# Three shift products of a fused long-convolution kernel: sums by accumulating DMA, one more inverse by eight, a borrowed gate buffer

## The chip, the cores and the metric

The program runs on one core of one Trainium2 chip. The metric is the device time of one execution in microseconds; the figure that counts is the median of several executions. Engines are named as the profile names them: PE (matmul), PEld (its weight loads), DVE, ACT, POOL, SP. SP, ACT and POOL also issue the DMAs.

## What is computed

Forward and backward of one block, sequence S = 2048, width D = 1024, hidden width F = 3584, all in bf16:

```python
xn = layernorm(q)
k_shift = sum_t k_pad[:, t:t+S, :] * shift_k[:, 3 - t]      # causal, four taps
kv = k_shift * v
y  = irfft(rfft(kv, 2S) * rfft(ssm_k, 2S))[:S] + kv * ssm_D   # long convolution
s  = xn * y
g  = silu(((xn @ w_gate) * (xn @ w_up)) @ w_down)
out = q + s * g
# outputs: out, and the gradients of q, k, v, shift_k, ssm_k, ssm_D and the three weights
```

The long convolution is done by matmuls with tables of sines and cosines (transforms of 128 points) and butterfly sums on DVE.

## The kernel before, in words

**The first 505 us** hold the part that the change touches. Two streams run interleaved there.

The *gate stream* multiplies xn by the gate and up weights. F is cut into NSL = 14 slabs of 256 columns; a slab is done in four *units* of 512 rows (`gu_unit`, L692; `turned_unit`, L664, for the slabs in `TURNED` = 2 to 6, 12, 13). A unit is four groups of eight 128x512 matmuls. Each group goes to one of two PSUM buffers (`psg`) and is copied by ACT to one half-row of a tile `gut`; after the fourth group ACT stores `gut` to DRAM (`GTd` or `GUd`). The product of the two halves (`multiply`, output `hN`, three buffers) is given to DVE after the first group of the next unit. A `gut` tile is free when its product is done and its store has landed. `gut_tile` (L658) hands them out: pool `fg` has two, and every third unit of slabs below 12 takes half of `U[5]` as a third. The last eight units are slab 12 rows 0 and 512, slab 13 rows 0 and 512, slab 12 rows 1024 and 1536, slab 13 rows 1024 and 1536; they are called units 1 to 8 below. In slabs that are not turned, pairs of `hN` are transposed on PE and copied by ACT to a tile `hT` (one buffer, pool `fg`), which SP stores (`turn_pair`, L730); the call is put off by five groups, so that of slab 11's last pair falls into unit 2.

The *convolution stream* is the generator `conv_forward` (L775). It goes over eight slices `ds` of 128 channels: transforms of the filter and of kv (PE matmuls to `psF`, ACT copies to `SP`, DVE sums `W`, `KX`, `HX`), the spectra's product on DVE, an inverse on DVE, and its last matmuls (`tail`, output `psI`). The inverse is `inv_dft` (L375), or `inv8` (L403) for slices in `INV8` = 4 to 7; `inv8` has more sums on DVE and leaves half as many matmuls to `tail`. For each pair of slices, `shift(dp)` (L793) makes kv: seven products and sums over 128x4096 elements on DVE and an eighth product with v. For dp = 1, 2, 3 it runs in one piece in the odd slice before, between the spectra's product and the inverse, with its inputs k and v loaded by `load_kv` at that slice's start; acc is `U[6]`, prod is `U[7]`, v is `U[4]`.

The order is fixed when the program is built. After each group, `tick` (L1020) advances the generator until the sum of its yielded weights reaches its share of `F_TOTAL`; a group of a turned slab counts `TURNED_TICK` = 0.958. DVE instructions of the convolution stay in program order (`PIN`), and every engine runs its own list in order. What is left of the convolution goes on beside the first matmuls of the next stage (`bm_first`, output `psbm`), up to about 560 us.

**After that** come the down projection, the gates' gradients, and the backward matmuls and convolutions, which the change does not touch. Late in them stands the one accumulating DMA that the kernel has: four times 1 MB from q onto out (L1772), DRAM to DRAM, issued by POOL.

Of the kernel before, what the change touches and what calls it, by code (L numbers as in the profile page):

```python
# [13 lines left out]
BF16 = mybir.dt.bfloat16  # L14
# [5 lines left out]
def build_kernel(  # L20
# [11 lines left out]
    nc = tc.nc  # L32
    P = 128
    _, S, D = A_q.shape
    F = B_w_gate.shape[1]
    assert (S, D, F) == (2048, 1024, 3584) and A_shift_k.shape[1] == 4
    NB = S // P
# [3 lines left out]
    NSL = F // SLW  # L41
# [16 lines left out]
    ADD, SUB, MUL = ALU.add, ALU.subtract, ALU.mult  # L58
# [6 lines left out]
    def st(out, in_):  # L65
        ins = nc.gpsimd.dma_start(out=out, in_=in_)
        if PINQ[0]:
            tc.keep_in_program_order(ins)
        return ins
# [6 lines left out]
    def cld_k(t, c, dp):  # L76

        rows = lambda u, n, a: bass.AP(kin.tensor, kin.offset + (1024 * c + 8 * u - 3 + a) * D + dp * 256,
                                       [[8 * D, n], [D, 11 - a], [1, 256]])
        for u, n, a in ((0, P, 0),) if c else ((16, P - 16, 0), (1, 15, 0), (0, 1, 3)):  # L80
            cld(t[u:u + n, a:], rows(u, n, a))
# [5 lines left out]
    def pool(name, bufs=1, side=None, space=None):  # L87
        kw = dict(name=name, bufs=bufs, reuse_waits="tile")
        if side:
            kw["side"] = side  # L90
        if space is not None:
            kw["space"] = space
        return tc.alloc_tile_pool(**kw)
# [10 lines left out]
    KSHd = dram.tile([4, P, NB, 256], BF16, name="KSHd")  # L104
# [9 lines left out]
    TURNED = (2, 3, 4, 5, 6, 12, 13)  # L114
# [16 lines left out]
    Wbc = const.tile([P, 4, D], BF16, name="Wbc")  # L131
# [77 lines left out]
    def pinned(ins):  # L209
        if PIN[0]:  # L210
            tc.keep_in_program_order(ins)
        newest[0] = ins

    def tt(o, a, b, op):
        pinned(V.tensor_tensor(o, a, b, op))  # L215
# [250 lines left out]
    def rowps(ps):  # L466
        return ps[:].rearrange("p r (c d) -> p r c d", c=2)
# [47 lines left out]
    U = [ua.tile([P, 4096], BF16, name=f"U{i}") for i in range(8)]  # L515
# [6 lines left out]
    fg = pool("fg", 2, side="right")  # L522
# [13 lines left out]
    kst = pool("kst", 1)  # L536
# [116 lines left out]
    turn_of = [0]  # L653
# [3 lines left out]

    def gut_tile(sl):  # L658
        turn_of[0] += 1
        if turn_of[0] % 3 == 0 and sl < NSL - 2:  # L660
            return U[5][:, 2048:4096].rearrange("p (a i f) -> p a i f", a=2, i=4)
        return fg.tile([P, 2, 4, SLW], BF16, name="gut")[:]

    def turned_unit(sl, b0, w, tick):  # L664
# [3 lines left out]
        for j in range(2):  # L668
            for a in range(2):
# [7 lines left out]
                hn[0] = nop  # L677
                tick(TURNED_TICK)
        cols = slice(b0 * P, b0 * P + 512)
# [85 lines left out]
    cv_gone = []  # L765
    ht_st = [None]
    EIGHT = ((0, 0), (0, 1), (6, 0), (7, 0), (7, 1))
    INV8 = (4, 5, 6, 7)
    SHIFT_W = 8 * 2.3

    conv_state = {"forward": True, "filters": True}
# [3 lines left out]
    def conv_forward():  # L775
        S_ = conv_state

        def load_kv(dp, c):
            S_["k", dp] = krow
            if dp > 0 or c == 0:  # L780
                for i in range(2) if dp == 0 else (c,):
                    cld_k(krow[:, i], i, dp)
            if dp > 0 or c == 1:
                for i in range(2) if dp == 0 else (c,):
                    v = U[4][:, 2048 * i:2048 * i + 2048].rearrange("p (a x) -> p a x", a=8)
                    cld_v(v, i, dp * 256, 256)
# [6 lines left out]
        def shift(dp):  # L793
            kv = cx.tile([P, NB, 256], BF16, name="kv")
            S_["kvt", dp] = kv
            k = S_.pop(("k", dp))
            wb = lambda j: Wbc[:, j:j + 1, dp * 256:(dp + 1) * 256].unsqueeze(1).to_broadcast([P, 2, 8, 256])
            room = cx.tile([P, 16, 256], BF16, name="KX")[:].rearrange("p a x -> p (a x)") if dp == 0 else U[7][:]
            acc, prod, v = [t.rearrange("p (c r d) -> p c r d", c=2, r=8) for t in (U[6][:], room, U[4][:])]
            with tc.issue_after(last.ins):  # L800
                tt(acc, k[:, :, 0:8, :], wb(3), MUL)
            yield 2.3
            for j in (2, 1, 0):
                tt(prod, k[:, :, 3 - j:11 - j, :], wb(j), MUL)
                yield 2.3
                tt(acc, acc, prod, ADD)
                yield 2.3
            tt(kv[:].rearrange("p (c r) d -> p c r d", c=2), acc, v, MUL)
            st(KSHd[dp], U[6][:].rearrange("p (b d) -> p b d", b=NB))
            yield 2.3  # L810
# [22 lines left out]
        def tail(ds):  # L833
# [5 lines left out]
            for rq in range(2):  # L839
                ps = (ps_tr if cv_gone else ps_cv).tile([P, 4, 256], F32, name="psI", tag="tr" if cv_gone else "psF")  # L840
                inv_quad(G, ps, rq, ds in INV8)
                pe_us[0] += 0.9 if ds in INV8 else 1.8
                nc.scalar.copy(out=yf.rearrange("p (c r) d -> p r c d", c=2)[:, 4 * rq:4 * rq + 4], in_=rowps(ps))
# [10 lines left out]
        cx = pool("cx", 1)  # L854
        cs = pool("cs", 1)
# [45 lines left out]
        sp = [half(0, S_["hx"], i, Dz[:, 0:P]) for i in range(2)]  # L901
        for ds in range(8):
            yield 0.5
            if ds % 2 == 1 and ds < 7:
                with tc.issue_after(S_["kst"].ins):
                    for c in range(2):
                        load_kv(ds // 2 + 1, c)
            D0 = Dz[:, ds * P:(ds + 1) * P]
            sph = []
            KX = cx.tile([P, 16, 256], BF16, name="KX")  # L910
            HX = cs.tile([P, 16, 256], BF16, name="HX", bufs=2)
            own_room = lambda X: X[:].rearrange("p a x -> p (a x)").bitcast(F32).rearrange("p (a x) -> p a x", a=8)[:, 0:4]
            eight = (ds, 1) in EIGHT
            if ds == 0:
                yield from transform(0, 1, sp, HX, own_room(KX), lambda i: sph.append(half(0, kvs(0), i)), nop)
            else:
                yield from transform(ds, 0, sp, KX, own_room(HX), lambda i: sph.append(half(ds, S_["hx"], i, D0)), nop)
                S_["kst"] = st(KFd[ds], KX[:])
            calls = []

            def behind():
                calls.append(0)
                if len(calls) % 2 == 0:
                    next(tl, None)
            room = cf.tile([P, 4, 256], F32, name="room", tag="hx")[:] if eight else None
            yield from transform(ds, int(ds > 0), sph, HX if ds else KX, room, nop1 if eight else lambda c: h_rows(ds + 1, c),
                                 behind)
            if ds == 0:
                S_["kst"] = st(KFd[0], KX[:])
            if eight:  # L930
                h_rows(ds + 1, 0)
            turned(HX, 1, 0, 1)
            yield 1.3
            if eight:
                h_rows(ds + 1, 1)
            if ds == 7:
                cf.release()
                S_["filters"] = False
            st(HFd[ds], HX[:])
            yield from product(KX, HX, KX, cs, False, 0)  # L940
            if ds % 2 == 1 and ds < 7:
                yield from shift(ds // 2 + 1)
            sp = []

            def ahead():
                if ds < 7:
                    sp.append(half(ds + 1, kvs(ds + 1), len(sp)))
            yield from (inv8 if ds in INV8 else inv_dft)(KX, HX, cs, ahead if ds % 2 == 0 else None, ahead)
            if ds % 2 == 1:
                ahead()  # L950
            S_["G", ds] = HX
            tl = tail(ds)
# [5 lines left out]
        kst.release()  # L958

    F_TOTAL = 4 * SHIFT_W + 3.0 + 8 * (0.5 + FWD4_W + 1.3 + PROD_W + INV_W) + 10.0 - 0.95 * 8 * (4 * 1.75 + 0.95 + 4 * 0.9)  # L960
    F_TOTAL += len(EIGHT) * (FWD8_W - 9.6 + 0.95 * 1.75) - 2.0
    F_TOTAL += len(INV8) * (INV8_W - INV_W + 0.95 * 1.8)
    conv = conv_forward()
# [50 lines left out]
    ps_cv = pool("ps_cv", 2, space=PSUM)  # L1014
    pump, drain, step = make_pump(conv, F_TOTAL)
    cnt = [-5]
    TURNED_TICK = 0.958
    NT = 24 * 8.0 + 33 - 16 * len(TURNED) * (1 - TURNED_TICK)

    def tick(by=1):  # L1020
        cnt[0] += by
        if cnt[0] == -4:
            pump((SHIFT_W + 4.05) / F_TOTAL)
        if cnt[0] >= -2:
            pump((SHIFT_W + (F_TOTAL - SHIFT_W) * (cnt[0] + 6.5) / (NT + 3.5)) / F_TOTAL)

    pump((SHIFT_W + 3.95) / F_TOTAL)
    for i_ in (4, 5):
# [267 lines left out]
    bpump, bdrain, _ = make_pump(conv_backward(), C_TOTAL)  # L1296
# [169 lines left out]
    for bp in range(2, 8):  # L1466
# [6 lines left out]
        with tc.issue_after(row_ld[0].ins):  # L1473
            if bp in (4, 5, 7):
                q = (4, 5, 7).index(bp)
# [206 lines left out]
    kpump, kdrain, _ = make_pump(dk_units(kw_), DK_TOTAL)  # L1682
# [70 lines left out]
    for g in range(1, 4):  # L1753
        for b in (4 * g, 4 * g + 2):
            end = b == NB - 2
            pss = [ps_x.tile([P, D], F32, name="psx") for i in range(2)]
            for n in range(12 if end else 14):
# [11 lines left out]
                elif b == NB - 4 and n in (0, 3, 6, 9):  # L1769
                    rows = slice(512 * (n // 3), 512 * (n // 3) + 512)  # L1770
                    with tc.issue_after(gu_mm[0].ins):
                        tc.keep_in_program_order(nc.gpsimd.dma_start(out=out_0.flatten_outer_dims()[rows, :],  # L1772
                                                                     in_=A_q.flatten_outer_dims()[rows, :], accum_op=ADD,
                                                                     max_dma_last_dim=4096))
# [82 lines left out]
```

## Time and profile before

| what | us |
|---|---|
| median of 3 executions | 1908.94 |
| the 3 executions | 1908.68, 1908.94, 1914.21 |
| the profiled execution, its own time | 1916.02 |
| its span, first to last instruction | 1914.2 |
| PE busy in 60 to 505 us (of 445) | 436.6 |
| DVE busy in 60 to 505 us (of 445) | 435.8 |
| PE busy in 560 to 1914 us (of 1354) | 1342.6 |

A "wait" below is idle time of an engine together with what ended it, as the profile infers it from semaphores. "Landing" is the time from a DMA's issue to its completion. The profiled execution is one execution; times inside it are counted from its first instruction.

### The profile page before, as it was taken

To read this page: it belongs to the slowest core of one execution; us is meant where nothing else is said; L and a number is where in the kernel's file an instruction comes from. 1 tells how busy PE (TensorE), PEld (TensorE's weight loads), DVE (VectorE), ACT (ScalarE), POOL (GpSimd) and SP (SyncE) were. 2 spreads that over 40 slices of the span, in tenths; PEclk is the share of its full clock that TensorE was granted. 3 is DMA by queue.
4 is the path that set the end of the run, shared out by engine and by line. 5 is a ranking of instruction groups with operands and counts; after the bars stand their busy time and mean duration, and the time that the engine had idled before them with its cause. 6 is when DMAs were issued, how large, how long until landed. Compare 5 with 4: busy or idle time off the path is not lost.

```text
span 1914.2 us, 27244 instructions
## 1 busy us (share of the span) xinstructions
PE 1886.6 (99%) x10815; PEld 1009.5 (53%) x10947; DVE 1544.5 (81%) x1701; ACT 611.7 (32%) x899; POOL 334.9 (17%) x465
## 2 busy tenths in 40 slices
PE   8999999999999999999999999999999999999998
PEld 4554555544444466666666656664444444444443
DVE  8999999999977546887999999999995206788843
ACT  5754545555232234332222222222222002011112
POOL 5121212101113210001021221211212101121121
PEclk9999999999999999999999999999999999999999
DMA  8777867759759998778987798685988999998997
GB/s 296 269 256 249 253 211 235 239 195 315 268 198 329 294 307 230 193 205 240 230 269 241 236 274 243 197 287 163 249 221 190 215 203 192 190 185 187 193 214 124
DMA packets 524447, 444.29 MB, mean 232 GB/s; under 512 B 356096, under 2 KB 451996, under 8 KB 512544
## 3 DMA queue, kind: packets, MB, share of 16 engines
q1 hardware_dynamic: 459680, 239.04, 51.0%
q0 software_dynamic: 41152, 174.15, 29.1%
q10 hardware_dynamic: 23488, 29.36, 4.4%
q8 instruction: 85, 1.39, 0.3%
q14 instruction: 42, 0.34, 0.1%
HBM read 171.85 MB, written 189.84 MB: 189 GB/s over the span
## 4 chain that ended last, share of the span: by engine, by line
PE 61%; DVE 11%; issue 9%; DMA 6%; POOL 1%; ACT 1%; SPq 0%; POOLq 0%; DVEq 0%; ACTq 0%
PE psb L1550 20%; PE psb L1533 10%; PE psb L1626 9%; PE psbm L1070 9%; PE psx L1688 7%; PE psg L672 3%; DMA dkT<-DKSHd 2%; DVE dkp L1285 2%; DMA dxna_t<-DXNAd 1%; PE psF L237 1%; DVE W L215 1%; DVE KX L215 1%; DVE dxn L215 1%; DVE HX L215 1%; DVE m L215 1%
## 5 line engine op out<-in xcount | busy, mean ns | idle before, releaser
L1550 PE MATMUL psb<-U,U 128*128 128x512 bf16 x1792 | 397.1, 379 | 0.0
L1688 PE MATMUL psx<-U,dgut 128*128 128x512 bf16 x1505 | 331.0, 379 | 1.6
L1688 PEld LDWEIGHTS <-dgut 128*128 128x128 bf16 x1792 | 175.3, 98 | 211.4
L1550 PEld LDWEIGHTS <-U 128*128 128x128 bf16 x1792 | 175.2, 98 | 198.0
L1533 PE MATMUL psb<-wdt,U 128*128 128x256 bf16 x1792 | 205.6, 273 | 0.0
L706 PE MATMUL psg<-wslab,U 128*128 128x512 bf16 x867 | 198.9, 379 | 5.5 <-DMA wslab<-in_B_w_gate_dram 2.4
L672 PE MATMUL psg<-U,wslab 128*128 128x512 bf16 x869 | 198.1, 381 | 3.7 <-ACT gut L674 2.3
L1533 PEld LDWEIGHTS <-U 128*128 128x128 bf16 x1792 | 175.2, 98 | 29.2
L215 DVE TENSOR_TENSOR W<-W 128x1024 f32<-128x1024 f32 (+1 forms) x183 | 180.3, 1002 | 4.0
L1626 PE MATMUL psb<-U,U 128*128 128x512 bf16 x797 | 176.1, 379 | 0.9
L1285 DVE SCALAR_TENSOR_TENSOR dkp<-dkT,kT 128x1024 bf16<-128x1024 bf16 (+2 forms) x64 | 78.3, 1224 | 115.9 <-DMA dkT<-DKSHd 114.1
L1555 ACT CAST wb<-psb 128x512 bf16<-128x512 f32 x112 | 65.6, 586 | 315.5 <-PE psb L1550 315.5
L1070 PE MATMUL psbm<-U,ht 128*128 128x512 bf16 x658 | 145.0, 379 | 0.7
L1626 PEld LDWEIGHTS <-U 128*128 128x128 bf16 x896 | 87.4, 98 | 104.3
L672 PEld LDWEIGHTS <-wslab 128*128 128x128 bf16 x896 | 87.4, 98 | 101.4 <-issue 3.4
L706 PEld LDWEIGHTS <-U 128*128 128x128 bf16 x896 | 86.1, 98 | 100.6 <-issue 3.0
L1720 ACT ACTIVATE dx_t<-dxn 128x1024 bf16<-128x1024 f32 x15 | 15.9, 1057 | 331.3 <-DVE dxn L215 331.3
L215 DVE TENSOR_TENSOR U<-U,dht 128x2048 bf16<-128x2048 bf16 x56 | 68.3, 1221 | 49.1 <-ACT dht L1535 48.9
L1070 PEld LDWEIGHTS <-ht 128*128 128x128 bf16 x672 | 65.7, 98 | 78.1
L1535 ACT CAST dht<-psb 128x512 bf16<-128x512 f32 x112 | 65.6, 587 | 116.2 <-PE psb L1533 115.9
L674 ACT CAST gut<-psg 128x512 bf16<-128x512 f32 x88 | 51.5, 587 | 87.5 <-PE psg L672 83.0
L1667 ACT CAST wbs<-psb 128x512 bf16<-128x512 f32 x51 | 29.9, 586 | 145.4 <-PE psb L1626 131.4
(268 smaller groups left out, 2456.1 us busy)
## 6 DMA issues: line engine op xcount, KB each, us to landing
DGd<-U SPq DMA_DIRECT2D x28, 1024.0 KB, 5.0
U<-GUd SPq DMA_DIRECT2D x14, 1024.0 KB, 9.7
out_dram<-wb SPq DMA_DIRECT2D x112, 128.0 KB, 3.7
GTd<-gut ACTq DMA_DIRECT2D x22, 512.0 KB, 5.1
ht<-HTd SPq DMA_DIRECT2D x18, 512.0 KB, 7.6
GUd<-gut ACTq DMA_DIRECT2D x17, 512.0 KB, 6.3
KFd<-KX POOLq DMA_DIRECT2D x8, 1024.0 KB, 4.9
HFd<-HX POOLq DMA_DIRECT2D x8, 1024.0 KB, 7.3
```

The costliest lines, as they stand in the source:

```text
L215: pinned(V.tensor_tensor(o, a, b, op))
L672: gu_mm[0] = nc.tensor.matmul(ps[:], w[:, dc, a, j * P:(j + 1) * P], XNT[b0 // 4][:, dc, :], start=(dc == 0), stop=(dc == DC - 1))
L674: nc.scalar.copy(out=gut[:, a, j], in_=ps[:])
L706: gu_mm[0] = nc.tensor.matmul(ps[:], XNT[q][:, dc, qi * P:(qi + 1) * P], w[:, dc].rearrange("p a f -> p (a f)"), start=(dc == 0), stop=(dc ...
L1070: mm = nc.tensor.matmul(ps[:, dh * 512:(dh + 1) * 512], ht(fc)[:, i * P:(i + 1) * P], WD[fc // 4][:, fc % 4, dh * 512:(dh + 1) * 512], sta ...
L1285: ins = V.scalar_tensor_tensor(prod[:].rearrange("p r d -> p (r d)")[:, lo:H], dkT[:, 0, lo:H], 1.0, kT[:, 0, 13 + m + lo:13 + m + H], op0 ...
L1533: nc.tensor.matmul(ps[:, x * SLW:(x + 1) * SLW], DBMT[2 * hf + g][:, dc, (b % 4) * P:(b % 4 + 1) * P], wdt[:, dc, :], start=(dc == 0), sto ...
L1535: nc.scalar.copy(out=dht[:, 2 * e:2 * e + 2].rearrange("p b f -> p (b f)"), in_=ps[:])
L1550: nc.tensor.matmul(ps[:], XN[b // 4][:, b % 4, dc * P:(dc + 1) * P], dgus[b // 8][:, :, b % 8], start=(b == 0), stop=(b == NB - 1))
L1555: nc.scalar.copy(out=wb[:, dc % 2].rearrange("p a f -> p (a f)"), in_=ps[:])
L1626: nc.tensor.matmul(ps, h[:, f, b, :], DBM[b // 4][:, b % 4, dh * 512:(dh + 1) * 512], start=(b == 0), stop=(b == NB - 1))
L1688: gu_mm[0] = nc.tensor.matmul(ps[:, dh * 512:(dh + 1) * 512], t[n][:, f, i * P:(i + 1) * P], WGU[n][:, f, dh * 512:(dh + 1) * 512], start= ...
```

## The change

Four edits, all in the forward stage.

1. `shift` is used for dp = 0 alone. For dp = 1, 2, 3 there is `shift_later`, in which the three sums acc += prod are DMAs from `U[7]` onto `U[6]` that POOL issues with `accum_op=ADD`. Its five steps (first product; product and DMA three times; product with v) are spread over an even slice and the odd one after it. `load_kv` moves to the start of the even slice.
2. Slice 2 joins `INV8`.
3. `gut_tile`: in slabs 12 and 13 every third unit takes the tile `hT` of pool `fg` (units 2, 5 and 8) as its `gut`.
4. `TURNED_TICK` becomes 1.0, and `F_TOTAL` loses the nine sums' weights.

```diff
     def gut_tile(sl):
         turn_of[0] += 1
+        if turn_of[0] % 3 == 0 and sl >= NSL - 2 and sl in TURNED:
+            return fg.tile([P, 4, 2, 2, P], BF16, name="hT", bufs=1)[:].rearrange("p q a i s -> p (q a i s)").rearrange("p (a i f) -> p a i f", a=2, i=4)
...
-    INV8 = (4, 5, 6, 7)
+    INV8 = (2, 4, 5, 6, 7)
...
+        def shift_later(dp):
...
+            tt(acc, k[:, :, 0:8, :], wb(3), MUL)
+            yield 2.3
+            for j in (2, 1, 0):
+                tt(prod, k[:, :, 3 - j:11 - j, :], wb(j), MUL)
+                nc.gpsimd.dma_start(out=U[6][:], in_=U[7][:], accum_op=ADD, max_dma_last_dim=4096)
+                yield 2.3
+            tt(kv[:].rearrange("p (c r) d -> p c r d", c=2), acc, v, MUL)
+            st(KSHd[dp], U[6][:].rearrange("p (b d) -> p b d", b=NB))
+            yield 2.3
...
-            if ds % 2 == 1 and ds < 7:
-                with tc.issue_after(S_["kst"].ins):
+            if ds % 2 == 0 and ds < 6:
+                with tc.issue_after(S_["kst"].ins) if ds else nullcontext():
                     for c in range(2):
                         load_kv(ds // 2 + 1, c)
+                later_kv = shift_later(ds // 2 + 1)
+            if ds % 2 == 1 and ds < 7:
+                yield next(later_kv)
...
+            if ds < 6:
+                for _ in range(2 - ds % 2):
+                    yield next(later_kv)
...
             yield from product(KX, HX, KX, cs, False, 0)
-            if ds % 2 == 1 and ds < 7:
-                yield from shift(ds // 2 + 1)
...
-            yield from (inv8 if ds in INV8 else inv_dft)(KX, HX, cs, ahead if ds % 2 == 0 else None, ahead)
+            inverse = (inv8 if ds in INV8 else inv_dft)(KX, HX, cs, ahead if ds % 2 == 0 else None, ahead)
+            yield next(inverse)
+            if ds % 2 == 1 and ds < 7:
+                yield next(later_kv)
+            yield from inverse
...
+    F_TOTAL -= 3 * 3 * 2.3
...
-    TURNED_TICK = 0.958
+    TURNED_TICK = 1.0
```

More of the change, by code (lines that the diff above doesn't have):

```diff
@@ L806, in shift @@
                 tt(acc, acc, prod, ADD)
+                yield 2.3
[3 more added lines that the diff above has]
+        def shift_later(dp):
+            kv = cx.tile([P, NB, 256], BF16, name="kv")
+            S_["kvt", dp] = kv
+            k = S_.pop(("k", dp))
+            wb = lambda j: Wbc[:, j:j + 1, dp * 256:(dp + 1) * 256].unsqueeze(1).to_broadcast([P, 2, 8, 256])
+            acc, prod, v = [t.rearrange("p (c r d) -> p c r d", c=2, r=8) for t in (U[6][:], U[7][:], U[4][:])]
+            tt(acc, k[:, :, 0:8, :], wb(3), MUL)
[3 more added lines that the diff above has]
+                nc.gpsimd.dma_start(out=U[6][:], in_=U[7][:], accum_op=ADD, max_dma_last_dim=4096)
                 yield 2.3
```

## The prediction

> **What bounds the kernel now.** I read the page first, then PE's waits from 60 us on, then the stretches.
>
> ```profile
> PE 1886.6 (99%) x10815; PEld 1009.5 (53%) x10947; DVE 1544.5 (81%) x1701; ACT 611.7 (32%) x899; POOL 334.9 (17%) x465
> ...
> engine line waited for: us in total, times, longest us
> PE psg L672 <- ACT gut L674: 2.3, 1, 2.3
> PE psF L237 <- DVE kv L215: 1.9, 2, 1.3
> PE psF L237 <- ACT SP L259: 1.3, 2, 0.9
> PE psg L706 <- ACT gut L708: 0.2, 1, 0.2
> PE psg L706 <- issue: 0.2, 1, 0.2
> ```
>
> PE is the bound, and all its waits after 60 us are these 5.9 us. The same view from 560 us to the end lists none. So a change to the forward stage can win PE's waits there, what the clock loses behind them, and matmuls that it removes: nothing else. The stretches show that DVE is as full as PE: 158.67 of 160 us in 140 to 300 and 138.56 of 140 in 300 to 440. That is why PE waits for kv and for SP copies (which wait for DVE to free SP).
>
> The longest wait is another matter, and its releaser has to be read with care:
>
> ```profile
> 449.32 1.93 ACT L740 COPY hT<-tr 128x1024 bf16<-128x1024 bf16 x2
> ...
> 452.88 0.59 ACT L674 CAST gut<-psg 128x512 bf16<-128x512 f32 x1 [1.14 <-PE psg L672]
> 453.50 0.38 ACTq L72 DMA_DIRECT2D GTd<-gut  x1
> ...
> 464.86 0.59 ACT L674 CAST gut<-psg 128x512 bf16<-128x512 f32 x1 [4.49 <-DVE hN L215]
> ...
> 456.17 0.68 DVE L215 TENSOR_TENSOR hN<-gut 128x1024 bf16<-128x1024 bf16 x1
> ...
> GTd<-gut ACTq DMA_DIRECT2D x1, 512.0 KB, 11.3
> ...
> 466.00:468.00 2.00, 2.00 (x7) 0.77 (x6) 1.97 (x2) 0.00 (x0) 0.00 (x0) 0.53 1.02 306
> 468.00:470.00 2.00, 2.00 (x12) 1.23 (x11) 1.97 (x3) 1.20 (x2) 0.00 (x0) 0.62 1.06 390
> ```
>
> At 464.86 ACT begins unit 4, whose gut buffer was unit 2's. Unit 2's product ran at 456.17, long before, so the named DVE product is not the cause: unit 2's store, issued at 453.2, took 11.3 us and landed at 464.5. PE idled 2.3 us, and then the clock column shows 0.53 and 0.62 for 2 us each, a half clock for 3.4 us (1.7 us lost). This one place cost 4.0 us.
>
> **The change part by part**, against the profiled execution (1916.0 us; span 1914.2 and 1.8 around it).
>
> *Slice 2 by eight.* tail's matmuls go from 32 to 16. Sixteen of them take 1.75 us in a row on PE, so **-1.7 us**. DVE gets two more 128x2048-sized sums, four more small pairs: by the rows for these shapes (2.29, 1.22, 0.68 us) inv8 is 16.3 us and inv_dft 9.5, so +6.8 us.
>
> *Nine sums off DVE.*
>
> ```profile
> L215 DVE TENSOR_TENSOR U<-U,U 128x4096 bf16<-128x4096 bf16 x9 | 20.6, 2288 | 0.2
> ...
> DMA to landing us min/median/max: 10.5/14.7/24.6
> ```
>
> 20.6 us go, 6.8 come: DVE is 13.8 us lighter, PE 1.7. Where PE waits decides what that is worth. In the changed program's instruction order I summed each engine's own work (rows x durations) up to the kv of pairs 1, 2, 3: DVE has 5.3, 4.6 and 11.5 us less ahead of them, but PE too has less ahead of its first use (5.1, 3.4 and 5.2 us), because the convolution is moved earlier against the gate groups (edit 4). So DVE gains only 0.2, 1.2 and 6.3 us on PE there. To this comes an idle 2.9 us of DVE at 130 us (it waits for ACT), which the products moved forward now fill. The waits of 0.5 and 1.3 us for kv should go, and of the later ones for SP most. Bounds 0 and -3.4 (1.9 + 1.3 + 0.2); I take **-2.4**.
>
> *The nine DMAs.* The trace has no accumulating DMA in SBUF. Nearest rows: the four of 1 MB onto out (landing 10.5 to 24.6 us, in a stretch with a DMA share of 0.94 to 1.28), and plain 1 MB stores here (4.9 us, KFd). The share here is 0.67 to 0.78 up to 440 us, so I take 10.5, the nearer end of the former. The first two of each pair have 25 us and more of DVE work until their result or U[7] is needed. The third has least: DVE's list between that product and kv is 17.1 us (by rows), so it is hidden under butterfly sums, to a landing of some 16 us; beyond that kv is late by the rest. POOL is 17% busy; an issue takes 1.0 us there, and the waits of these DMAs stand behind stores that wait for older DVE work, so nothing is held up. KSHd's store waits for the third DMA at POOL, and behind it are hN stores of products that DVE reaches later still. The moved k and v loads (some 10.5 us to land) have 28 us of DVE work until the first product. DMA share: 46.3 MB of POOL's queue cost 30.8% of 440 us, 2.9 us per MB; 9 MB at one to two times that are 6 to 13% more. **0**, with +25 as the far end (rival 3).
>
> The Trainium skill, "DMA: Bandwidth & Descriptors", section "Anatomy of one DMA — SWDGE (gpsimd) path", gives 2.0 us + bytes/436e3 per us for a DMA from this queue: 4.4 us for 1 MB as my estimate by that page. The four rows above are two to six times that. By the page rival 3 would have no chance at all; by the rows it has one.
>
> *The third gate buffer.* Unit 4 no longer shares unit 2's buffer, so the 4.0 us above go. But hT is also turn_pair's tile, and slab 11's last turn_pair stands in unit 2, after hT has been handed out as unit 2's gut. In the changed order on ACT its two copies (before: at 449.32, in the middle of unit 2, waiting for nothing late) stand after the second copy of unit 3, and wait for **unit 2's store to land**. Behind them on ACT are unit 3's third copy and all later ones; PE has two psg buffers and can run only to the end of unit 3. Count from T = 452.9, the end of unit 2's matmuls, with L the store's landing: issue T+0.4, seen at T+0.7+L, two copies 1.9, third copy 0.6, so PE starts unit 4 at T+L+3.3 instead of T+6.9. A wait of **L - 3.6 us**. Before, the wait began only above L = 9 (11.3 gave 2.3).
>
> L is the open size: 11.3 here before, 7.4 median for 435 to 505 us, 6.0 median of all such stores. I take 6.0, since HFd's 1 MB store and the YFd store, which lay beside it, are issued some 4 us earlier against unit 2 in the changed order. That gives a wait of 2.4 us. Does the clock drop behind it? One idle of 2.3 us did so here, one of 1.3 us at 292 did not: I take half of 1.7, so +3.3. Against the profiled execution -4.0 + 3.3 = -0.7.
>
> The Trainium skill, "TensorE: Matmul & The Clock Gate", section "Why this matters for your kernels", advises against idle gaps over about 3 us, one window of idle halving the clock. The 2.3 us in this trace did it already, so the measurement decides; by the page a 2.4 us gap would cost no clock, 0.9 us less in the sum.
>
> *TURNED_TICK.* It moves convolution work between slabs; that is in the counts above. Its end lies at the same matmul as before, and PE does not wait for the last psI today.
>
> **Sum.** -1.7 - 2.4 - 0.7 = -4.8 us: 1911.2 for the profiled execution. That one is 7.1 us above the median, and of three others two lie within 0.3 us at 1908.7 and 1908.9, one at 1914.2. The 4.0 us at unit 4 hang on one DMA's landing and are the largest piece that can differ; I take them as absent in the median. Then the median gains 1.7 + 2.4 and pays 3.3: 1908.94 - 0.8 = **1908.1 us**. A measurement of this kernel can tell about 0.3% (5.7 us) from no change, so this is no change.
>
> **The rivals.**
>
> 1. *All waits go.* If unit 2's store lands within 3.6 us, ACT's copies are not late. For: other stores of this tile land in 2.9 us. Against: 7.7, 11.3 and 11.4 around that place. Then 1908.9 - 1.7 - 3.4 = 1903.8, or 1899.8 if the median holds the 4.0 us as the profile does. Chance 0.24.
> 2. *Slower: the copies of hT hold up ACT.* The mechanism above with a large L. It eats the other gains (4.1 us) from L = 6.0 with a clock drop, and with 11.3 us, as seen, PE idles 7.7 us and loses 1.7 to the clock: 1908.9 - 4.1 + 9.4 = 1914.2. From L = 11.8 it is over 0.3%. For: the measured 11.3. Against: the neighbours' earlier issue. Chance 0.2.
> 3. *The third DMA makes kv late.* With a landing of 24.6 us kv is 8.5 us late three times, 25.5 us, of which DVE's lighter list gives back 13.8: 1908.9 - 1.7 + 11.7 = 1918.9. For: the row's maximum. Against: it was measured in a fuller stretch. Chance 0.06.
>
> Forecast (waits partly exchanged): 0.5, its own range 1904 to 1912. The range 1901 to 1914 takes in rival 2's and most of rival 1's. Faster by over 0.3% (below 1903.2): most of rival 1's half with the 4.0 us, and a forecast that gains it too, 0.2. Slower by over 0.3%: rival 3 and half of rival 2, 0.16. Within: 0.64.
>
> **What would show it.** Right: in unit 3 an idle stretch of ACT before the hT copies, ended by unit 2's GTd store, and PE idle before unit 4; no wait of 2 us at unit 4's first copy; no PE wait for kv; DVE idle a few us more; accumulating DMAs landing in 8 to 14 us, psI matmuls 16 fewer. Wrong: hT copies that wait for nothing, kv waiting for a DMA, or waits of PE after 505 us.

## The result and the profile after

| | before | changed |
|---|---|---|
| median of 11 executions, us | 1909.51 | 1923.63 |
| lowest to highest | 1908.68 to 1914.32 | 1913.67 to 1937.09 |
| the profiled execution / its span | 1916.02 / 1914.2 | 1937.09 / 1935.3 |

The ratio is 1.0068, 95% interval 1.0053 to 1.0083: slower by 0.7%, outside the predicted range, and spread over 23 us where the kernel before had 6 in the runs beside it. (On other chips the kernel before spreads more too: 1908.5 to 1928.0 us in 35 executions on one, up to 1925.2 on another. Of its 106 executions beside the runs below, 8 took 1920 us or more; of the changed kernel's 19 in all, 12 did.) Medians and ratios in this document leave out executions over 1.5% above the fastest of the same kernel, one each of no_sums, third_dve, early_sum, best and two_repairs, at 1941.7 to 1972.1 us.

First the page's busy times and PE's waits from 60 us on, changed kernel (columns: engine, line, what it waited for; us in total, times, longest).

```profile
PE 1893.0 (98%) x10798; PEld 1010.2 (52%) x10931; DVE 1529.8 (79%) x1702; ACT 611.6 (32%) x899; POOL 345.4 (18%) x474
...
PE psb L1577 <- DVE U L215: 9.5, 2, 7.4
PE psg L674 <- ACT gut L676: 4.5, 1, 4.5
PE psb L1577 <- ACT dht L1562: 3.7, 1, 3.7
PE psg L708 <- ACT U L710: 3.3, 1, 3.3
PE psg L674 <- ACT U L710: 2.7, 1, 2.7
...
PE psF L237 <- DVE kv L215: 0.4, 2, 0.2
```

What the change set out to do is there: DVE is 14.7 us less busy, the waits for kv went from 1.9 to 0.4 us and those for SP from 1.3 to nothing. But PE waits 25.6 us in all after 60 us, and three of the waits are new ones in gate units (2.7 us at 85, 3.3 at 403, 4.5 at 468); 13.2 us more end between 940 and 963 us, in code that the change leaves alone. ACT's timeline shows what the three gate waits are: the releaser in the brackets is a store each time.

```profile
82.60 1.01 ACT L761 COPY hT<-tr 128x1024 bf16<-128x1024 bf16 x1 [3.38 <-DMA HTd<-hT]
...
401.28 1.93 ACT L742 COPY hT<-tr 128x1024 bf16<-128x1024 bf16 x2 [4.35 <-DMA HTd<-hT]
...
465.89 1.93 ACT L742 COPY hT<-tr 128x1024 bf16<-128x1024 bf16 x2 [4.86 <-DMA GTd<-hT]
```

ACT stands before a copy to hT until hT's last store has landed; the copies that free PE's two psg buffers stand behind it. The landings of those three stores, changed kernel (KB each, us from issue to landing), and of the first two before:

```profile
HTd<-hT SPq DMA_DIRECT2D x1, 256.0 KB, 8.1
...
HTd<-hT SPq DMA_DIRECT2D x1, 512.0 KB, 16.8
...
GTd<-hT ACTq DMA_DIRECT2D x1, 512.0 KB, 8.2
```

```profile
HTd<-hT SPq DMA_DIRECT2D x1, 256.0 KB, 2.5
...
HTd<-hT SPq DMA_DIRECT2D x1, 512.0 KB, 3.4
```

The first (74 us) is in flight beside the k and v loads that the change moved to slice 0; the second (384 us) was issued 2.0 us after an accumulating transfer and 0.2 us after HFd's store:

```profile
382.37 1.19 POOL L824 DMA_DIRECT2D U<-U  x1 [2.87 <-DVE U L215]
383.11 1.17 POOL L66 DMA_DIRECT2D Hd<-hN  x1
384.18 0.66 POOL L66 DMA_DIRECT2D HFd<-HX  x1
...
384.39 0.37 SPq L61 DMA_DIRECT2D HTd<-hT  x1
```

Behind each of these waits PE's clock (third column from the right) is halved for 3.4 us:

```profile
86.00:88.00 2.00, 2.00 (x5) 0.68 (x5) 2.00 (x4) 0.42 (x1) 0.00 (x0) 0.50 0.91 269
404.00:406.00 2.00, 2.00 (x6) 0.76 (x5) 1.78 (x3) 0.19 (x1) 0.67 (x1) 0.50 0.92 256
468.00:470.00 2.00, 1.44 (x3) 0.55 (x4) 1.17 (x2) 0.80 (x2) 0.18 (x1) 0.56 0.63 201
```

The accumulating transfers themselves behave much as forecast: issue 1.2 us, landing 9.1 us, and PE's waits for kv are down to 0.4 us.

```profile
L824 POOL DMA_DIRECT2D U<-U x9: 1186/1221/1230, 115.1 to 382.4; - x9
...
DMA to landing us min/median/max: 8.2/9.1/11.0
```

### The profile page after: what moved, and what is told of

The parts are those of the page before. It is cut to its first block, busy times and chain, and to the rows that moved or that the text cites. A ratio compares the mean times of both kernels' runs of the same rounds, so it can differ in the third digit from the quotient of the medians.

```text
span 1935.3 us, 27222 instructions
## 1 busy us (share of the span) xinstructions
PE 1893.0 (98%) x10798; PEld 1010.2 (52%) x10931; DVE 1529.8 (79%) x1702; ACT 611.6 (32%) x899; POOL 345.4 (18%) x474
## 4 chain that ended last, share of the span: by engine, by line
PE 86%; DVE 6%; DMA 4%; issue 2%; ACT 1%; SPq 0%; POOL 0%; DVEq 0%; ACTq 0%; POOLq 0%
PE psx L1715 20%; PE psb L1577 17%; PE psbm L1097 10%; PE psb L1653 9%; PE psb L1560 9%; PE psg L674 8%; PE psg L708 6%; PE psF L237 3%; DVE W L215 1%; DMA vl<-in_A_v_dram 1%; DMA HTd<-hT 1%; DVE KX L215 1%; DVE m L215 1%; PE psY L1256 1%; PE psY L448 1%
## 5 line engine op out<-in xcount | busy, mean ns | idle before, releaser
L1577 PE MATMUL psb<-U,U 128*128 128x512 bf16 x1792 | 401.1, 381 | 13.2 <-DVE U L215 9.5
L215 DVE TENSOR_TENSOR W<-W 128x1024 f32<-128x1024 f32 (+1 forms) x189 | 186.5, 1003 | 4.0
L215 DVE TENSOR_TENSOR W<-SP 128x1024 f32<-128x1024 f32 x64 | 74.5, 1218 | 2.8 <-ACT SP L298 1.9
```

The source lines that it names most:

```text
L1577: nc.tensor.matmul(ps[:], XN[b // 4][:, b % 4, dc * P:(dc + 1) * P], dgus[b // 8][:, :, b % 8], start=(b == 0), stop=(b == NB - 1))
```

## The experiments

Theory A: the added and moved transfers, and the loan of hT, make stores land late whose tile ACT needs next; ACT works in order, so PE runs dry, and the clock halves. Theory B: the loss belongs to something else, the forward order as a whole or the late stretches. "Before" is the kernel before on the same chip, in the same runs; ratios are to it, with the 95% interval.

| run | what it is | before, us | run, us | ratio (interval) |
|---|---|---|---|---|
| again | the changed kernel | 1910.1 | 1920.8 | 1.0055 (1.0032 to 1.0078) |
| no_third | changed, without the loan of hT | 1910.1 | 1916.6 | 1.0031 (1.0019 to 1.0042) |
| only_third | before, with the loan alone | 1910.1 | 1913.4 | 1.0015 (1.0006 to 1.0025) |
| sums_dve | changed, the nine sums on DVE | 1910.1 | 1925.0 | 1.0072 (1.0060 to 1.0084) |
| late_loads | changed, first k and v loads later | 1912.3 | 1920.6 | 1.0038 (1.0015 to 1.0062) |
| no_sums | changed, the nine transfers left out | 1912.3 | 1917.0 | 1.0018 (0.9992 to 1.0044) |
| third_dve | changed, each third sum on DVE | 1912.3 | 1926.5 | 1.0068 (1.0030 to 1.0105) |
| only_inv8 | before, with slice 2 by eight | 1912.3 | 1910.8 | 0.9987 (0.9963 to 1.0010) |
| units36 | changed, hT lent to units 3 and 6 | 1912.1 | 1933.7 | 1.0111 (1.0083 to 1.0139) |
| early_sum | changed, third product and transfer earlier | 1912.1 | 1933.2 | 1.0109 (1.0071 to 1.0146) |
| best | units36, early_sum and late_loads in one | 1912.1 | 1928.4 | 1.0089 (1.0058 to 1.0119) |
| inv8_units36 | before, slice 2 by eight and hT lent to units 3 and 6 | 1912.1 | 1908.7 | 0.9978 (0.9955 to 1.0002) |
| two_repairs | changed, late loads, no loan, one sum on DVE | 1913.9 | 1924.9 | 1.0073 (1.0044 to 1.0102) |
| two_repairs_again | the same | 1909.8 | 1915.1 | 1.0029 (1.0004 to 1.0054) |
| two_repairs_no_dma | the same, its eight transfers left out | 1909.8 | 1915.8 | 1.0030 (1.0008 to 1.0052) |

### The changed kernel twice more

> The changed kernel once more, for a second profile. Theory A (the added and moved transfers make neighbouring stores land late, ACT's copies of hT wait for them, PE runs out of free buffers): PE waits of 2 to 5 us near 85, 403 and 468 us are there again, and the stretch at 905 to 965 us, where all transfers took 30 us in the first profile and PE waited 13.2 us, is not part of it: there the wait is under 2 us, and the profiled execution takes 1913 to 1922 us. Theory B (the backward stretch belongs to the change): the waits at 940 to 965 us are 8 us or more again, and the profiled execution is at 1930 us or more. Median 1916 to 1928 by either.

> A third profile of the changed kernel. The waits near 85, 403 and 468 us are there again, each 2 to 5 us. In the late stretches: 3 us or more of PE waits if these come with the change, as in two of two so far; under 2 us in some executions if they are chance.

The three gate waits are there in all three profiles, the late one is not. The second profile took 1934.7 us, which only theory B had expected, but not at the place that B named: it waited 5.1 us at 1904 us and nothing at 940 to 965. The third (1918.0 us) has 0.3 us of late waits. PE's waits of the third in the forward stage:

```profile
PE psg L674 <- ACT gut L676: 4.4, 1, 4.4
PE psg L674 <- ACT U L710: 3.3, 1, 3.3
PE psg L708 <- ACT U L710: 2.7, 1, 2.7
PE psF L237 <- DVE kv L215: 0.4, 2, 0.2
```

So the three waits come back with the program, and the late ones come and go.

### The loan of hT

```diff
-        if turn_of[0] % 3 == 0 and sl >= NSL - 2 and sl in TURNED:
-            return fg.tile([P, 4, 2, 2, P], BF16, name="hT", bufs=1)...
```

> The changed kernel without its third gate buffer in slabs 12 and 13. If that buffer (hT as gut, with slab 11's two hT copies held on ACT until unit 2's store has landed) is what costs, the 4.5 us wait at 468 us and the half clock behind it go, at most 2.5 us come back at unit 4, and the median is 3 to 6 us below the changed kernel's 1923.6. If my forecast of an even exchange was right, it is within 2 us of it. If the moved transfers cost, the waits near 85 and 403 us stay in the profile.

> The kernel before with the third gate buffer in slabs 12 and 13 alone. By the wait L - 3.6 us (L the landing of unit 2's store): with L = 6, 2.4 us and half a clock loss against some 0 to 4 us that go, so 1908 to 1913; with L = 11, as in both profiles so far or near, PE idles 7 us and the clock halves for some us behind, 1914 to 1919. A rival: L is no more than 4 here, then nothing waits, and the median is 1907 to 1910.

Put alone into the kernel before (only_third) the loan costs 3.3 us, clear of noise. Taken from the changed kernel (no_third) it gives 4.2 us back by the medians (1920.8 to 1916.6), but there the two intervals overlap. The profile of only_third, wait and landing:

```profile
PE psg L674 <- ACT gut L676: 3.8, 1, 3.8
```

```profile
GTd<-hT ACTq DMA_DIRECT2D x1, 512.0 KB, 7.5
```

L - 3.6 gives 3.9. In the changed kernel's three profiles L is 8.2, 7.9 and 8.2, and the wait 4.5, 4.2 and 4.4. In all nine profiles of kernels with this loan (L from 7.5 to 9.0) the rule held to 0.2 us; L did not (I took 6.0). no_third's wait did not go but moved: unit 3 now waits 3.3 us for unit 1's store, which takes 13.0 us beside HFd's and YFd's.

### The moved loads

```diff
-            if ds % 2 == 0 and ds < 6:
-                with tc.issue_after(S_["kst"].ins) if ds else nullcontext():
+            if ds in (2, 4):
+                with tc.issue_after(S_["kst"].ins):
...
+            if ds == 0:
+                with tc.issue_after(hd_st[0].ins):
+                    for c in range(2):
+                        load_kv(1, c)
+                later_kv = shift_later(1)
```

> The changed kernel with the first early pair of loads (k and v for pair 1) queued on POOL behind slab 1's last hN store, near 89 us instead of 66 us. Theory A: beside the loads, the HTd store of 74 us took 8.1 us instead of 2.5, and ACT's next hT copy waited for it; so that store lands in 2 to 4 us again, the PE wait near 85 us (2.6 to 3.1 us, half clock for 2.6 us behind it) goes, and the median falls by 3 to 5 us against the changed kernel run beside before (1920.8 to 1923.6). Rival: the landing is long for another reason (slice 0's KSHd and the ssm_k load, which were there before), then nothing moves. Price to watch: the loads have only some 18 us until the first product; if they are late, DVE waits for k near 108 us.

The store of 74 us lands in 2.2 us, and the wait near 85 us is gone (no wait of PE between 60 and 395 us is over 0.4 us):

```profile
HTd<-hT SPq DMA_DIRECT2D x1, 256.0 KB, 2.2
```

That settles where this wait comes from. In the time the gain is not seen for certain: the ratio is 1.0038 against the changed kernel's 1.0055 and 1.0068, with intervals that overlap, and this profile has a late wait of 5.7 us at 948.

### The accumulating transfers

```diff
-                nc.gpsimd.dma_start(out=U[6][:], in_=U[7][:], accum_op=ADD, max_dma_last_dim=4096)
```

> The changed kernel with the nine accumulating transfers left out and nothing in their place, so the sums over the taps are not formed (k_shift is one product only). It tells what holds the HTd store near 384 us for 17 us. If it is the accumulating transfer issued 2 us ahead, the store lands in 8 us or less and the PE wait near 403 us (3.3 to 3.9 us) is gone. If it is the HFd store that the new order puts 0.2 us ahead of it, the landing stays above 12 us and the wait stays at 2 us or more. The waits near 85 us (loads) and 468 us (hT as gut) stay by both.

> The changed kernel with its nine sums as DVE additions in the places where the accumulating transfers stood; all else stays. If the accumulating transfers crowd the stores (theory A, part one), the wait near 403 us goes, the one near 85 us (moved k and v loads, theory A, part two) stays. DVE has 20.6 us more to do there, and 6.8 us more than the kernel before: if DVE's load decides, PE waits for kv and SP copies grow by 4 to 7 us over those of before, and the median is 1920 or more; if the transfers decide, it is below 1919.

> The changed kernel with each pair's third sum on DVE; the first two stay accumulating transfers. Theory A: the third is the one that is issued just ahead of the HFd and HTd stores; without it the PE wait near 403 us goes, DVE gets 6.9 us of sums back (as much as before plus 0 to 1 us), PE waits for kv and SP copies grow by 0 to 2 us, and the median falls by 2 to 5 us. Rival: DVE's load costs what the stores win (sums_dve was at 1925), median unchanged or above.

Without them (no_sums) the HFd store is still issued 0.2 us ahead of HTd's, and both are quick; ACT's copies at 398 us wait for nothing:

```profile
HFd<-HX POOLq DMA_DIRECT2D x1, 1024.0 KB, 4.5
HTd<-hT SPq DMA_DIRECT2D x1, 512.0 KB, 5.5
```

So the accumulating transfer is what makes 16.8 out of 5.5, and the wait at 403 us with it. Sums on DVE in the same places (sums_dve, third_dve) remove that wait too (the store lands in 2.9 and 3.0 us), but PE then waits for kv and SP copies: 7.8 us in sums_dve, 4.8 in third_dve, against 3.2 before. The weights that set their order do not count these sums, so DVE is late against it, and putting the sums back into this order is no repair: I had expected third_dve to be 2 to 5 us faster than the changed kernel, and neither median is below the changed kernel's (1920.8 to 1923.6).

### Slice 2 by eight

```diff
-    INV8 = (4, 5, 6, 7)
+    INV8 = (2, 4, 5, 6, 7)
```

> The kernel before with slice 2 among those inverted by eight, and nothing else. PE has 16 matmuls less, 1.75 us; DVE 6.8 us more, in a stretch in which it is 99% busy. If DVE's slack before its first use on PE covers it, the median is 1908 (1.7 below before); if PE has to wait, up to 5 us of waits for kv and SP copies come on top, 1910 to 1914.

Median 1.5 us below before, which the interval does not tell from nothing. PE's waits for SP grow from 1.3 to 3.1 us, that for kv shrinks from 1.9 to 1.0: 0.9 us of the 1.75 is given back.

### Repairs that fell

```diff
-        if turn_of[0] % 3 == 0 and sl >= NSL - 2 and sl in TURNED:
+        if turn_of[0] % 3 == 1 and sl >= NSL - 2 and sl in TURNED:
...
             room = cf.tile([P, 4, 256], F32, name="room", tag="hx")[:] if eight else None
+            if ds % 2 == 1 and ds < 7:
+                yield next(later_kv)
```

The first two lines are units36, the lines behind them early_sum (the third product, which stood after the second transform of an odd slice, now stands ahead of it); best has both, and the late loads.

> The changed kernel with hT lent to units 3 and 6 instead of 2, 5 and 8, so that slab 11's last two hT copies come ahead of the loan and wait for nothing late, and unit 4 takes unit 1's gut buffer, stored long before. If the wait at 468 us is the two hT copies behind unit 2's store, it goes altogether (no wait over 1 us from 440 to 505 us), and the median falls by 4 to 8 us against the changed kernel (1920.8 to 1923.6). Rival: the next wait takes its place (unit 3's copies behind the HTd store, or unit 5 behind unit 2's store with its 13 us landing), 2 us or more at unit 3 or 5, median no more than 2 us lower. The waits near 85 and 403 us stay by both.

> The changed kernel with the third product and its accumulating transfer one transform earlier in the odd slice, some 10 us ahead of the HFd store. If the HTd store near 384 us lands late because it shares the engines with that accumulating transfer (without the transfers it took 5.5 us), it lands in 5 to 10 us, the PE wait near 403 us (2.9 to 3.9 us) is gone or under 1 us, and the median is 3 to 5 us below the changed kernel's. Rival: KSHd's store, which now comes free at the same time, takes the transfer's place beside HFd, and the landing stays above 12 us.

> All three repairs in one: first loads behind slab 1's last hN store, third sum one transform earlier, hT lent to units 3 and 6. If the three waits are the whole cost of the change, what is left are its gains: 1.75 us of matmuls, 3.2 us of waits for kv and SP copies and, in part of the executions, the wait of some 4 us at unit 4. Then the median is 3 to 7 us below the kernel before of the same chip. If the transfers cost in other places as well (the late loads of backward, more spread), it is level with before or above.

units36 met its rival: unit 3's copies to hT wait for slab 11's last HTd store, which lands in 12.5 us here.

```profile
468.87 1.07 ACT L676 CAST hT<-psg 128x512 bf16<-128x512 f32 x2 [10.40 <-DMA HTd<-hT]
```

early_sum frees the store that landed in 16.8 us (it lands in 4.7, and the wait at 403 is gone), but KSHd's store, HFd's and the next pair's k loads, at the first place YFd's too, now fall together at 160 to 190 and 282 to 305 us, and stores from hN land late there (the one in the line below took 23.2 us). DVE then stands before the product that needs the tile, ACT and kv behind it; PE waits 5.9 and 6.1 us:

```profile
302.96 0.69 DVE L215 TENSOR_TENSOR hN<-gut 128x1024 bf16<-128x1024 bf16 x1 [5.88 <-DMA HTd<-hN]
```

best, with all three repairs, has these waits and the one of units36 (4.0, 6.6 and 8.0 us; its only profile is of the execution of 1957.0 us). The same amount of transfers, moved elsewhere, found another tile. That fits theory A, though no run took away the transfers beside these new late stores; as repairs all three failed, 16 to 22 us above the kernel before.

### Without accumulating transfers: slice 2 by eight and the loan to units 3 and 6

> The kernel before with slice 2 by eight and hT lent to units 3 and 6, with the sums where they were, on DVE. It tells whether the accumulating transfers are worth anything beside the other two edits: if DVE's load is what PE waits for, this one keeps 3 to 5 us of waits for kv and SP copies and is level with before to 2 us below; the kernel with all three repairs then beats it by 2 us or more. If they are level, the transfers bring nothing.

3.4 us below before, with an interval that just reaches no change; all its six executions lie between 1907.3 and 1912.9. Its waits for SP and kv are 4.3 us, 0.5 us is left at the loan, and 1.9 us fell on a load at 730 us. No kernel with accumulating transfers had a median near it: best, on the same chip, lies 20 us above it. So the accumulating transfers, in the orders tried, brought nothing in time, though they end the waits for kv and SP copies.

### Two repairs, with and without the transfers

```diff
-                nc.gpsimd.dma_start(out=U[6][:], in_=U[7][:], accum_op=ADD, max_dma_last_dim=4096)
-                yield 2.3
+                if j or dp < 3:
+                    nc.gpsimd.dma_start(out=U[6][:], in_=U[7][:], accum_op=ADD, max_dma_last_dim=4096)
+                else:
+                    tt(acc, acc, prod, ADD)
+                yield 2.3 if j or dp < 3 else 4.6
```

The loan is taken out, the first loads come late as in late_loads, and pair 3's third sum alone is on DVE. The second kernel leaves out the eight accumulating transfers that remain (k_shift lacks those sums).

> The changed kernel without the loan of hT, with the first loads behind slab 1's last hN store, and with pair 3's third sum alone on DVE (its weight counted in the order). Theory A: no wait near 85 us, none near 403 us; what stays is unit 4 behind unit 2's store, with its landing of 10 to 13 us in the new order a wait of 1 to 4 us. Then the median is 1906 to 1911 and level with before. If the late stretches cost regularly in kernels with accumulating transfers, it is 1914 or more although the forward waits are gone.

> The kernel with two repairs once more, as the partner of the next one on the same chip. Its profile of before was clean (4.7 us at unit 4, nothing late, 1910.6 us), its median 1926. If that median was the chip's of that hour, it is 1908 to 1914 now; if the eight accumulating transfers or the new order cost regularly, 1918 or more.

> The kernel with two repairs and its eight accumulating transfers left out, with nothing in their place (k_shift lacks those sums); the order of all else is the same. If these transfers are what costs in most executions, its median is within 3 us of the kernel before or under it, and 8 us or more under its partner's. If it is the new order (what meets what on the transfers' engines in the late stretches), it is within 3 us of its partner.

The waits at 85 and 403 us are gone, as expected. What stays in the gate units is unit 3 behind unit 1's store, which takes 15.1 us in the second of these runs (14.3 in the first):

```profile
456.53 1.07 ACT L674 CAST gut<-psg 128x512 bf16<-128x512 f32 x2 [7.39 <-DMA GTd<-gut]
```

The profiled executions took 1910.6 and 1910.4 us, but the medians are 11 and 5 us above before. On one chip the kernel with the eight transfers and the one without them are level (1915.1 and 1915.8; 1908.8 to 1934.9 and 1909.9 to 1929.0), where before lies between 1908.4 and 1918.4. Five of the 12 executions of two_repairs_again lie at 1908.8 to 1911.0 us, level with before, where the changed kernel never came below 1913.7: in these the forward loss is gone. And since the kernel without the transfers spreads as far, what makes this larger spread is not the accumulating transfers themselves but something that the two share. Slice 2 by eight is shared, but alone it spreads no more than before (only_inv8, 1907.5 to 1918.7, where before reached 1928.0 on that chip). What is left is the new order. This is by elimination: which of the moves makes it (the loads, the spread products, the weights, TURNED_TICK) was not tried.

### The late stretches

> The kernel before once more, for its late stretches (900 to 970 us and 1860 to 1915 us). If these waits belong to the chance of how SP's transposing loads and POOL's loads meet, a profile of before shows landings of 25 us or more in one of them in some executions, and PE waits of 3 us or more there in a slow one (1925 us and more). If they belong to the change, all profiles of before show under 2 us of PE waits after 505 us.

> As for the repeat of the kernel before: a third profile of it, with the same two readings.

Both repeats of before are quiet after 505 us (1909.0 and 1911.4 us). No profile caught one of its executions of 1920 us or more, so whether those have the same late losses stays open. In the 20 profiles the late loss has a pattern. At about 900 us SP issues transposing loads (U from GTd) while POOL issues a burst of DYFd, A, B and v. In the first profile of the changed kernel and in its third (the second line is the median of two loads, 6.9 and 39.7 us in the first, 6.2 and 10.3 in the third):

```profile
A<-DYFd POOLq DMA_DIRECT2D x1, 1024.0 KB, 32.5
...
U<-GTd SPq DMA_TRANSPOSE x2, 23.3
```

```profile
A<-DYFd POOLq DMA_DIRECT2D x1, 1024.0 KB, 10.3
...
U<-GTd SPq DMA_TRANSPOSE x2, 8.2
```

| second such load is issued, against POOL's DYFd store | profiles | its landing, us |
|---|---|---|
| 0.8 to 2.6 us after (before, only_third, only_inv8, inv8_units36) | 6 | 15.2 to 17.6 |
| 1.2 to 1.6 us ahead | 9 | 10.1 to 11.4 |
| 0.5 to 1.0 us ahead (changed, late_loads, early_sum, best; units36) | 5 | 39.7, 31.5, 34.9, 31.4; 15.4 |

In the four that crawled (over 30 us) PE waited 6.3 to 13.9 us between 900 and 1000 us, in units36 1.9 us, in the 15 others not at all. What sets the distance can be read too. POOL's burst follows the first of the two loads by 3.3 to 3.5 us in all 20 profiles, and the second load is issued as soon as SP is done with issuing the first. That took 1.9 to 2.3 us in the nine profiles, 2.5 to 2.9 in the five and 4.3 to 6.0 in the six. So the distance follows from how long SP's first issue takes, and the crawl may come from whatever slows that issue rather than from the distance itself.

The first of the last two transposing loads (U from HT2d, near 1860 us) and the last of the four accumulating transfers from q onto out pair up likewise: issued within 0.8 us of each other, in 6 profiles (that of before among them), the load lands in 26 to 39 us and the time from PE's last matmul to the end is 7.8 to 11.4 us; in the 14 others, 1.8 us or more apart, it is 17 to 27.5 and 3.4 to 5.7 us. The second profile of the changed kernel:

```profile
out_dram<-in_A_q_dram POOLq DMA_DIRECT2D x1, 1024.0 KB, 35.2
...
U<-HT2d SPq DMA_TRANSPOSE x1, 36.8
```

Kernels with the new order have the first pair at 0.5 to 1.6 us ahead, where a shift of half a microsecond goes with over 20 us of landing in four cases of five; the old order has it 0.8 us or more on the other side. This is read from 20 profiles. No run moved one of these issues alone, and why such a pair crawls is open.

## Why the prediction was wrong

- **"The nine DMAs ... 0."** This step failed. I asked whether their own results would come in time, and they do (landing 9.1 us against my 10.5; rival 3 did not happen). I put their cost at nothing without asking what lands late beside them: HTd's store took 16.8 us instead of 3.4, which cost 3.3 us of PE and about 1.4 us of clock. no_sums shows it. The Trainium skill says in "DMA: Bandwidth & Descriptors", section "Issuing engines are not separate DMA queues", that transfers issued by ACT, SP and POOL run on the same 16 engines and interleave; the 16.8 and 5.5 us of one SP store with and without a POOL transfer agree.
- **"The moved k and v loads ... have 28 us of DVE work."** The same omission: the loads were in time, the store beside them was not. That cost 2.7 us of PE and about 1.6 us of clock; late_loads shows it.
- **The third gate buffer: right mechanism, mis-sized term.** L was 8.2 us, not 6.0. The 6.0 was not the median of such stores either: the page of before has 22 stores from gut to GTd with a median of 5.1 us, so that the neighbourhood of this one store decided, not the median. (Unit 2's store of before was issued at 453.5 us, as its row says, and landed at 464.8, not at 453.2 and 464.5; the count from T does not change by it.) HFd's and YFd's stores did move away from unit 2's store, and onto unit 1's (13.0 us). The wait was 4.5 us with about 1.5 us of clock against my 3.3 in all: rival 2, whose price for L = 8.2 would have been 4.6 + 1.7.
- **"I take them as absent in the median."** Nearly: the execution of before at 1909.0 us still has 1.5 us of that wait, without a clock drop, and the one at 1911.4 us has 2.2 us and a half clock. But unit 4 was not most of what set the first profile apart. Of the 7.0 us between it and the one at 1909.0, 4.3 lie at the end: from PE's last matmul to the end it took 7.8 us, in both repeats 3.5.
- **kv and SP: right.** -2.8 us measured against -2.4.
- **Slice 2: right in what it removes.** psI matmuls went from 192 to 176. What that is worth in time no run told from nothing (only_inv8).
- **"Waits of PE after 505 us"** stood among what would make the forecast wrong, and came. I had taken the later stages as untouched because their instructions are. What the profiles show is that the time at which two transfers meet there differs with the order before them, and that long landings go with it; what causes what there is open.

The sum, an estimate from the first profile's waits: to the forecast of -0.8 come 4.3 (85 us), 4.7 (403) and 2.7 (6.0 instead of 3.3 at 468), together +10.9, or 1919.8 us from the median of before. The quiet third profile lies 9.0 us above the quiet repeat of before on the same chip (1917.99 and 1909.04). The rest of the median, about 4 us in one set of executions and 1 us in the other, and the spread up to 1937 us are what the late stretches would account for. Of executions without a profile only the granted clock is known: 0.992 to 0.996 in those over 1925 us, 0.998 and 0.999 in the two fastest (1913.7 us). These two lie 5 us above the lowest of before, not 11, so not every execution pays the three waits and their half clocks in full.

## What to carry to other kernels

When work moves from an engine to a transfer, do not only ask whether its result comes in time: list the stores that will share the next 10 us with it, and for each the tile that it holds and the in-order engine that needs this tile next. A single-buffered tile with a store behind it (hT here) is where such transfers were paid for in this kernel, and moving them moved the bill to other tiles. A tile that is lent out makes all its other users wait for the borrower's store: price the loan by the landing of that store in the new order, not by the median of all stores.

## What the runs showed of the hardware

- An accumulating transfer of 1 MB from SBUF to SBUF landed in 8.2 to 11.0 us in the three profiles of the changed kernel and cost POOL 1.2 us to issue.
- One and the same 512 KB store (HTd, near 384 us) took 3.2 to 3.8 us in the kernels with the old order, 5.5 beside a 1 MB store (no_sums), and 16.2 to 17.4 with a 1 MB accumulating transfer in front as well (six profiles).
- An idle PE of 2.2 us (third profile of before), 2.3 us (first profile of before) and 2.7 us (85 us, changed) was followed by a half clock; one of 2.6 us (85 us, second profile), 2.7 us (403 us, third) and 3.3 us (464 us, no_third) was not. All idles over 3.4 us after 60 us, in 20 profiles, were. Apart from those that ran into the end of the program, each half clock lasted 3.4 us or two or three times that. The Trainium skill, "TensorE: Matmul & The Clock Gate", section "Why this matters for your kernels", warns of gaps over about 3 us; here 2.2 us was enough in one case and 3.3 us was not in another.
- A transposing load issued within a microsecond ahead of a burst from POOL landed in 31 to 40 us in four profiles of five; issued 1.2 to 1.6 us ahead, in 10.1 to 11.4 us in all nine. Why is open.
